# Scores and values of a unit in one place each, and k of batch 1 turned by one DMA transpose, in a fused attention and GEGLU kernel

## The chip, the cores and the metric

The kernel runs on one core of one Trainium2 chip. The metric is the device time of one execution in microseconds (us), the median of several runs. Beside it stands one profiled execution, from which all durations below come.

## The reference

Two stages follow each other. The first is attention in which each query sees its neighbours closer than 16 positions, and for each block of 32 positions one summary key (the maximum over the block) with one summary value (the mean). The second is a gated feed-forward layer over the 3072 tokens, with a gated residual.

```python
# q, k, v: 4 batches x 8 heads x 768 positions x 64
k_sum = k.reshape(B, H, nb, block, D).max(axis=3)        # block = 32, nb = 24
v_sum = v.reshape(B, H, nb, block, D).mean(axis=3)
mask_l = np.abs(pos[:, None] - pos[None, :]) < window    # window = 16
scores_s = scale * einsum(q, k_sum) + np.log(block)
a = softmax(concatenate([where(mask_l, scale * q @ k.T, -1e9), scores_s]))
x = a @ concatenate([v, v_sum])          # to 3072 tokens x 512
g, val = x @ w_gate, x @ w_val           # 512 -> 1536
ffn = (gelu(g) * val) @ w_out            # 1536 -> 512
out = x + sigmoid(x @ w_res) * ffn
```

## The kernel before

The work is cut into eight units, two per batch: a unit is half a batch's positions, thus 384 tokens (`TU`), with all 8 heads. `NP` = 4 head pairs, `HT` = 6 tiles of 64 queries (`QT`) in a unit.

**Attention.** For a tile of 64 queries the keys stand in one stationary matrix of 128 columns in `kW`: the tile's own 64 keys, 16 of the tile after, 16 of the tile before (the rims, written by `k_rims`, L245 and L246), and the 24 block maxima (`k_blocks`, L237 and L241). One matmul per tile and head gives the scores (L317). ScalarE takes their exponentials into P (L334 or L337), VectorE multiplies by a mask (L341), and a matmul with P as the stationary side gives values and the sum of weights (L355). `av_end` divides (L373, L375) into `xn`. `xt_dma` (L385) turns `xn` into `xT` by a DMA transpose; in the first two units TensorE turns it (`xt_step`).

**Feed-forward.** Twelve steps `fo_step`, one for each 128 of the 1536 columns: four matmuls g and four vv (L395), a Gelu on ScalarE (L400) and a product on VectorE (L401) into `gvT`. Then `res_step` (r, L433, with a Tanh, L436) and `ffn_step` (f, L443), and `end_step` writes the output rows from the SP queue (L456).

**Order.** The order on each engine is the order of the program text, written out by hand. While unit u ends (`mid_out`, in unit 0 `first_out`), the attention of unit n = u + 1 is interleaved with its r and f: two head pairs of scores, r, a third of f, two pairs of values, two of scores, more of f, two of values. `s_step(n, hp)` does one head pair; its scores take two PSUM banks with 384 of 512 columns used. The names `ps_mm` (4 banks), `ps_s` (2), `ps_t` and `ps_o` (1 each) are the PSUM pools; `MM2` and `TO2` name pairs of banks.

**Preparing the next batch.** Loads that change float32 to bfloat16 are issued from POOL (GpSimd), in order; a DMA waits until the one eight before it has landed. For batches 2 and 3, k is loaded with positions on the partitions (`load_k_nat`, eight DMAs, L121), turned by one DMA transpose from the SP queue (`turn_k`, L131), and POOL writes the rims of all pairs at once. For batch 1, k is loaded by one DMA (`load_k`, L89) and turned on TensorE at the first step of unit 1 (`turn_all`, 64 small transposes, L220); ScalarE places it (`k_place`, L252) and VectorE writes blocks and rims, a pair at a time at steps 0, 2, 4, 6. In unit 1, step 5, SP turns q of batch 1 (`turn_q`, L136), TensorE sums v over blocks (`vsum_grp`, L290), ScalarE copies the sums to `vpart` (L294), POOL issues four small DMAs to `vsum` (L296) and copies them into the value tiles (`vsum_bc`, L302).

Of the kernel before, what the change touches and what calls it, by code (L numbers as in the profile page):

```python
# [8 lines left out]
F32 = mybir.dt.float32  # L9
BF16 = mybir.dt.bfloat16  # L10
# [5 lines left out]
def kernel(  # L16
# [11 lines left out]
    nc = tc.nc  # L28
# [25 lines left out]
    wpool = ctx.enter_context(tc.tile_pool(name="wpool", bufs=1))  # L54
    qk = ctx.enter_context(tc.tile_pool(name="qk", bufs=1))
    work = ctx.enter_context(tc.tile_pool(name="work", bufs=3))
    ppool = ctx.enter_context(tc.tile_pool(name="ppool", bufs=4))
    upool = ctx.enter_context(tc.tile_pool(name="upool", bufs=2))
    ps_mm = ctx.enter_context(tc.tile_pool(name="ps_mm", bufs=4, space=bass.MemoryType.PSUM))
    ps_s = ctx.enter_context(tc.tile_pool(name="ps_s", bufs=1, space=bass.MemoryType.PSUM))  # L60
# [17 lines left out]
    q_nat = const.tile([128, NQ, DM], BF16, name="q_nat")  # L78
    vext = [const.tile([128, NT, H, VP], BF16, name=f"vext{i}") for i in range(2)]
    vsum = [const.tile([128, DM], BF16, name=f"vsum{i}") for i in range(2)]  # L80
    vpart = const.tile([128, DM], BF16, name="vpart")
    w_gate = wpool.tile([128, KO, DFF], BF16, name="w_gate")
    w_val = wpool.tile([128, KO, DFF], BF16, name="w_val")
# [55 lines left out]
    with tc.manual_schedule():  # L139
# [182 lines left out]
        def s_step(u, hp, st, banks=None, tiles=None):  # L322
            if tiles:
                s, banks = tiles, True
            elif banks:
                s = [p.tile([128, 512], F32, tag=tag, name="s") for p, tag in banks]
            else:
                s2 = ps_s.tile([128, 2, 512], F32, tag="s", name="s")
                s = [s2[:, hh] for hh in range(2)]
            s_mm(u, hp, [x[:, 0:TU] for x in s])  # L330
            P = ppool.tile([128, 2, HT, QT], BF16, tag="P", name="P")
            if banks:
                for hh in range(2):
                    nc.scalar.activation(P[:, hh].rearrange("p t q -> p (t q)"), s[hh][:, 0:TU], AF.Exp,  # L334
                                         scale=scale, bias=bias_t[:])
            else:
                nc.scalar.activation(P.rearrange("p a t q -> p a (t q)"), s2[:, :, 0:TU], AF.Exp,  # L337
                                     scale=scale, bias=bias_t[:])
            if u:
                Pf = P.rearrange("p a t q -> p (a t) q")  # L340
                nc.vector.tensor_mul(Pf, Pf, maskt.unsqueeze(1).to_broadcast([128, 2 * HT, QT]))  # L341
            st["P", hp] = P

        MM2 = ((ps_mm, "mm"),) * 2
        TO2 = ((ps_t, "t"), (ps_o, "ao"))
# [31 lines left out]
        def xt_step(u, ko, st, pool, tag, copy=nc.vector.tensor_copy):  # L377
            xp = pool.tile([128, TU], BF16, tag=tag, name="xp")
            for sub in range(NSUB):
                nc.tensor.transpose(xp[:, sub * 128:(sub + 1) * 128],  # L380
                                    st["xn"][:, ko, sub, :], ident[:])
            copy(st["xT"][:, ko, :], xp[:])

        def xt_dma(ko, st):
            nc.sync.dma_start_transpose(out=st["xT"][:, ko].rearrange("d (s k) -> d s k", k=128),  # L385
                                        in_=st["xn"][:, ko].rearrange("p s d -> p (s d)"))
# [6 lines left out]
        def gv_mm(ps, w, st, fo, kos):  # L393
            for ko in kos:
                nc.tensor.matmul(ps[:, 0:TU], w[:, ko, fo * 128:(fo + 1) * 128], st["xT"][:, ko, :],  # L395
                                 start=(ko == 0), stop=(ko == KO - 1), skip_group_check=True)

        def gv_end(gvT, fo, g, vv):
            ge = work.tile([128, TU], F32, tag="ge", name="ge")
            nc.scalar.activation(ge[:], g[:, 0:TU], AF.Gelu)  # L400
            nc.vector.tensor_mul(gvT[:, fo, :], ge[:], vv[:, 0:TU])  # L401

        def mm_tile(name):
            return ps_mm.tile([128, 512], F32, tag="mm", name=name)
# [13 lines left out]
            gv_end(gvT, 0, g, vv)  # L418

        def fo_last_two(st, gvT):  # L420
            g = [mm_tile("g"), mm_tile("g")]
            for i in range(2):
                gv_mm(g[i], w_gate, st, FO - 2 + i, range(KO))
            for i in range(2):
                vv = mm_tile("vv")
                gv_mm(vv, w_val, st, FO - 2 + i, range(KO))
                gv_end(gvT, FO - 2 + i, g[i], vv)

        def res_step(st, sub):
            ss = slice(sub * 128, (sub + 1) * 128)  # L430
# [117 lines left out]
        xt_step(0, 2, st, **t_turn)  # L548
        gv_part(0, 1)
        gv_mm(gv[1][0], w_gate, st, 1, (0, 1))  # L550
        xt_step(0, 3, st, **o_turn)
        gv_part(0, 2)
        gv_mm(gv[1][1], w_val, st, 1, (0, 1))
        gv_part(0, 3)
# [27 lines left out]
        def pool_after(x):  # L582
            nc.gpsimd.tensor_copy(gate2[:], x)
# [31 lines left out]

        def mid_out(u, st, gvT, nst):
            n = u + 1
            other = dict(pool=ps_t, tag="t")
            s_step(n, 0, nst)
            s_step(n, 1, nst, TO2)  # L620
            res_step(st, 0)
            res_step(st, 1)
            ffn_step(st, gvT, 0, 0, 4)
            av_step(n, 0, nst)
            xt_dma(0, nst)
            av_step(n, 1, nst, **other)
            xt_dma(1, nst)
            s_step(n, 2, nst)
            s_step(n, 3, nst, MM2)
            if n % 2 == 0:  # L630
                pool_after(nst["P", 3][0:1, 0, 0, 0:1])
                for i in range(2, 4):
                    vsum_bc(n // 2, 3 * i, 3 * i + 3, nc.gpsimd)
            ffn_step(st, gvT, 0, 4, FO)
            ffn_step(st, gvT, 1, 0, 3)
            av_step(n, 2, nst)
            xt_dma(2, nst)
            av_step(n, 3, nst, **other)
            xt_dma(3, nst)
            end_step(u, st, 0)  # L640
            ffn_step(st, gvT, 1, 3, FO)
            res_step(st, 2)
            end_step(u, st, 1)
            ffn_step(st, gvT, 2, 0, FO)
            end_step(u, st, 2)
# [9 lines left out]
        for u in range(NU):  # L655
            b, half = u // 2, u % 2
            nb = b + 1
            if half == 0 and nb == 1:
                k_sb[nb] = k_tile()
                load_k(nb, k_sb[nb], 0, 1)  # L660
                v_loads(nb)
                load_q_nat(nb)
            if u:
                gvT = upool.tile([128, FO, TU], BF16, tag="gvT", name="gvT")
            for fo in range(0 if u else 2, FO):
                if u == 0 and fo == 2:
# [24 lines left out]
                if half == 1 and nb < B:  # L691
                    if fo == 0:
                        v_rims(nb, 0, HT)
                        if nb > 1:
                            pool_after(st["xT"][0:1, KO - 1, 0:1])
                            load_q_nat(nb)
                    if fo == (5 if nb == 1 else 1):
                        turn_q(nb, 0)
                        turn_q(nb, 1)
                        vsum_grp(nb, ps_t, "t")  # L700
                        for i in range(2):
                            vsum_bc(nb, 3 * i, 3 * i + 3, nc.gpsimd)
                    if nb == 1:
                        if fo == 0:
                            tk = turn_all(k_sb[nb])
                        if fo in (0, 2, 4, 6):
                            hp = (2, 0, 1, 3)[fo // 2]
                            k_place(nb, hp, tk[hp])
                    elif 2 <= fo < 2 + NP:
                        k_blocks(nb, fo - 2)  # L710
            if u == NU - 1:
                last_out(u, st, gvT)
            else:
                nst = new_unit()
                (mid_out if u else first_out)(u, st, gvT, nst)
                st = nst

# [29 lines left out]
```

The softmax here doesn't subtract the row's maximum and nothing guards it: scores larger than these inputs give would overflow.

## Time and profile before

| what | value |
|---|---|
| median of 3 runs | 256.26 us (256.26 to 256.71) |
| the profiled execution | 256.39 us |
| its span, first to last instruction | 254.6 us |
| mean granted TensorE clock | 0.998 |
| TensorE (PE) matmul busy | 246.6 us, 97% |
| VectorE (DVE) busy | 159.4 us, 63% |
| ScalarE (ACT) busy | 129.6 us, 51% |
| GpSimd (POOL) busy | 97.3 us, 38% |
| DMA moved | 29.34 MB, mean 115 GB/s |

Times inside the span count from its first instruction. PE is the matmul row, PEld the weight loads beside it. A line such as "L443 PE MATMUL f<-w_out,gvT" means: line 443, engine, operation, what is written and from what. "Idle before" is the time in which that engine had nothing to do ahead of the instruction, and the name behind the arrow is what ended it. An engine that is not the bottleneck may be idle at no cost.

### The profile page before, as it was taken

The numbers are of one execution on the slowest core, as the hardware profiler recorded it, in microseconds if no ns is written. First come the engines' busy times: TensorE is split into PE (matmuls) and PEld (weight loads), VectorE is DVE, ScalarE is ACT, GpSimd is POOL, SyncE is SP. The second block draws the span as 40 slices with busy tenths as digits, with TensorE's granted clock in tenths as the row PEclk, the third lists the DMA queues.
The fourth block names the chain that finished last, engine by engine and source line by source line (L and its number), as shares of the span: only waits on it lengthen the run. The fifth ranks groups of instructions, "written<-read, shape, count | busy, mean of one in ns | idle before, by whom it ended". The sixth has DMA issues, their size and how long they took to land.

```text
span 254.6 us, 5847 instructions
## 1 busy us (share of the span) xinstructions
PE 246.6 (97%) x2303; PEld 139.7 (55%) x2328; DVE 159.4 (63%) x364; ACT 129.6 (51%) x216; POOL 97.3 (38%) x128
## 2 busy tenths in 40 slices
PE   6999999999999999999999999999999999999994
PEld 2676555565545665446544665446545555456544
DVE  6985796397667544858567544958567544854424
ACT  8885468366572337353572337254572337353320
POOL 8895542361506970274406970274404000000000
PEclk9999999999999999999999999999999999999999
DMA  5999999999404999399404999289604400230003
GB/s 80 177 182 197 197 205 207 175 176 222 61 19 121 159 150 150 56 161 171 103 18 120 162 155 153 49 162 170 104 18 115 98 3 0 50 139 0 3 1 124
DMA packets 98107, 29.34 MB, mean 115 GB/s; under 512 B 83224, under 2 KB 94944, under 8 KB 97984
## 3 DMA queue, kind: packets, MB, share of 16 engines
q0 software_dynamic: 68352, 14.76, 66.3%
q1 hardware_dynamic: 29728, 14.21, 25.7%
q8 instruction: 18, 0.29, 0.5%
q14 instruction: 9, 0.07, 0.1%
HBM read 29.36 MB, written 6.29 MB: 140 GB/s over the span
## 4 chain that ended last, share of the span: by engine, by line
PE 93%; DVE 5%; issue 2%; DVEq 0%
PE g L395 25%; PE vv L395 24%; PE f L443 23%; PE r L433 8%; PE s L317 3%; PE ao L355 3%; PE vs L282 1%; PE ao L367 1%; PE tp L220 1%; PE vs L290 1%; DVE ks L237 1%; PE xp L380 1%; DVE o L452 1%; DVE th L449 1%; PE gv L395 1%
## 5 line engine op out<-in xcount | busy, mean ns | idle before, releaser
L401 DVE TENSOR_TENSOR gvT<-ge,vv 128x384 bf16<-128x384 f32 x95 | 52.2, 552 | 48.1 <-PE vv L395 43.9
L400 ACT ACTIVATE ge<-g 128x384 f32<-128x384 f32 x95 | 46.7, 491 | 67.3 <-DVE gvT L401 34.8
L395 PE MATMUL g<-xT,w_gate 128*128 128x384 bf16 x380 | 78.0, 326 | 0.0
L395 PE MATMUL vv<-xT,w_val 128*128 128x384 bf16 x380 | 77.8, 326 | 0.0
L443 PE MATMUL f<-w_out,gvT 128*128 128x512 bf16 x262 | 62.7, 379 | 1.5 <-issue 1.1
L395 PEld LDWEIGHTS <-w_gate 128*128 128x128 bf16 x384 | 37.1, 98 | 26.2 <-issue 1.4
L395 PEld LDWEIGHTS <-w_val 128*128 128x128 bf16 x384 | 37.6, 98 | 24.7
L443 PEld LDWEIGHTS <-gvT 128*128 128x128 bf16 x276 | 25.7, 98 | 29.5
L107 POOL DMA_DIRECT2D vext<-in_v_dram x32 | 24.1, 777 | 15.0 <-DMA w_out<-in_moe_w_out_dram 5.6
L436 ACT ACTIVATE th<-r 128x512 f32<-128x512 f32 x24 | 13.5, 607 | 27.6 <-PE r L433 27.6
L449 DVE SCALAR_TENSOR_TENSOR th<-th,f 128x512 f32<-128x512 f32 (+2 forms) x26 | 16.6, 640 | 14.4 <-PE f L443 14.4
L341 DVE TENSOR_TENSOR P<-P,maskt 128x768 bf16<-128x768 bf16 x28 | 16.2, 580 | 11.0 <-ACT P L337 6.1
L433 PE MATMUL r<-w_res,xT 128*128 128x512 bf16 x88 | 22.7, 380 | 0.4
L302 POOL COPY vext<-vsum 32x1536 bf16<-32x1536 bf16 x12 | 17.2, 1464 | 13.0 <-DMA vsum<-vpart 12.9
L452 DVE SCALAR_TENSOR_TENSOR o<-th,xn 128x512 f32<-128x512 f32 (+2 forms) x26 | 18.2, 701 | 0.9
L375 DVE TENSOR_TENSOR xn<-ao,rz 128x384 bf16<-128x384 f32 x32 | 17.8, 557 | 1.1
L337 ACT ACTIVATE P<-s,bias_t 128x768 bf16<-128x768 f32 x17 | 15.3, 901 | 4.5 <-PE s L317 4.3
L127 POOL DMA_DIRECT2D q_nat<-in_q_dram x18 | 15.8, 899 | 0.9 <-issue 0.7
L334 ACT ACTIVATE P<-s,bias_t 128x384 bf16<-128x384 f32 x30 | 15.7, 579 | 0.0
L237 DVE TENSOR_REDUCE ks<-kW 128x24 bf16<-128x768 bf16 x16 | 15.1, 943 | 0.0
L433 PEld LDWEIGHTS <-xT 128*128 128x128 bf16 x96 | 8.8, 98 | 9.9
L373 DVE RECIPROCAL rz<-ao 128x6 f32<-128x6 f32 x32 | 6.1, 191 | 10.9 <-PE ao L355 10.0
(90 smaller groups left out, 187.1 us busy)
## 6 DMA issues: line engine op xcount, KB each, us to landing
out_dram<-o SPq DMA_DIRECT2D x23, 256.0 KB, 2.2
vext<-in_v_dram POOLq DMA_DIRECT2D x32, 96.0 KB, 6.4
q_nat<-in_q_dram POOLq DMA_DIRECT2D x18, 128.0 KB, 6.4
w_gate<-in_moe_w_gate_dram POOLq DMA_DIRECT2D x6, 256.0 KB, 8.9
w_val<-in_moe_w_val_dram POOLq DMA_DIRECT2D x6, 256.0 KB, 9.3
w_out<-in_moe_w_out_dram POOLq DMA_DIRECT2D x3, 512.0 KB, 14.4
k_nat<-in_k_dram POOLq DMA_DIRECT2D x16, 96.0 KB, 5.8
vext<-vext SPq DMA_DIRECT2D x6, 144.0 KB, 5.4
```

What stands on the lines that cost most here:

```text
L107: nc.gpsimd.dma_start(out=vext[b % 2][0:QT, :, h, 0:D], in_=v[b, h].rearrange("(t p) d -> p t d", p=QT))
L237: nc.vector.tensor_reduce(out=ks.rearrange("d (t n) -> d t n", n=2), in_=kw[:, :, 0:QT].rearrange("d t (n w) -> d t n w", w=BLK), axis=myb ...
L302: eng.tensor_copy(vext[b % 2][96:128, lo:hi, :, 0:D], src)
L341: nc.vector.tensor_mul(Pf, Pf, maskt.unsqueeze(1).to_broadcast([128, 2 * HT, QT]))
L375: nc.vector.tensor_mul(xn, ao[:, :, :, 0:D], rz.to_broadcast([128, NSUB, 2, D]))
L395: nc.tensor.matmul(ps[:, 0:TU], w[:, ko, fo * 128:(fo + 1) * 128], st["xT"][:, ko, :], start=(ko == 0), stop=(ko == KO - 1), skip_group_ch ...
L400: nc.scalar.activation(ge[:], g[:, 0:TU], AF.Gelu)
L401: nc.vector.tensor_mul(gvT[:, fo, :], ge[:], vv[:, 0:TU])
L433: nc.tensor.matmul(r[:], st["xT"][:, ko, ss], w_res[:, ko, :], start=(ko == 0), stop=(ko == KO - 1))
L443: nc.tensor.matmul(st["f", sub][:], gvT[:, fo, ss], w_out[:, fo, :], start=(fo == 0), stop=(fo == FO - 1), skip_group_check=True)
L449: nc.vector.scalar_tensor_tensor(th[:, cs], th[:, cs], 1.0, f[:, 0:n], ALU.add, ALU.mult)
L452: nc.vector.scalar_tensor_tensor(o.rearrange("p (k d) -> p k d", d=128), th[:, cs].rearrange("p (k d) -> p k d", d=128), 0.5, x, ALU.mult, ...
```

## The change

Four things are changed.

- Unit 2 and later: `mid_out` computes all scores of the next unit in one place, before r (`s_all`), and all values in one place, after the first f (`av_all`). The 24 (pair, tile) scores of a head fill banks of 512 columns: six banks in all, two each from `ps_mm`, `ps_s` and `ps_t` with `ps_o`. P becomes one tile, `p_all`, that all units share, in place of a pool of four.
- k of batch 1 is loaded as for the later batches, by eight DMAs, and turned by one DMA transpose, which SP issues at the end of unit 0's steps, ahead of `first_out`. POOL writes its rims at step 6 of unit 1, VectorE its blocks at steps 6 to 9.
- `fo_last_two` issues each Gelu behind its g in the text.
- The last `xT` copy of unit 0 goes from ScalarE to VectorE.

```diff
+    p_all = const.tile([128, 2, NP * HT, QT], BF16, name="p_all")
...
-            P = ppool.tile([128, 2, HT, QT], BF16, tag="P", name="P")
+            P = p_all[:, :, hp * HT:(hp + 1) * HT]
...
+        def s_all(u):
...
+            for i in range(3):
+                if i == 0:
+                    s = [ps_mm.tile([128, 512], F32, tag="mm", name="s") for _ in range(2)]
+                elif i == 1:
+                    s2 = ps_s.tile([128, 2, 512], F32, tag="s", name="s")
+                    s = [s2[:, hh] for hh in range(2)]
+                else:
+                    s = [p.tile([128, 512], F32, tag=tag, name="s") for p, tag in TO2]
+                for j in range(8):
+                    hp, t = divmod(8 * i + j, HT)
+                    tt = half * HT + t
+                    for hh in range(2):
+                        ps = slice(hh * 64, hh * 64 + 64)
+                        nc.tensor.matmul(s[hh][:, j * QT:(j + 1) * QT], kw[ps, tt, hp, :],
+                                         qt[ps, tt // 2, hp, (tt % 2) * QT:(tt % 2 + 1) * QT],
+                                         start=True, stop=True, skip_group_check=True)
+                js = slice(8 * i, 8 * i + 8)
+                m = maskt.unsqueeze(1).to_broadcast([128, 8, QT])
+                for hh in range(1 if i == 1 else 2):
+                    if i == 1:
+                        nc.scalar.activation(p_all[:, :, js].rearrange("p a j q -> p a (j q)"), s2[:], AF.Exp,
+                                             scale=scale, bias=bias_t[:])
+                    else:
+                        nc.scalar.activation(p_all[:, hh, js].rearrange("p j q -> p (j q)"), s[hh][:], AF.Exp,
+                                             scale=scale, bias=bias_t[:])
+                for hh in range(2):
+                    nc.vector.tensor_mul(p_all[:, hh, js], p_all[:, hh, js], m)
+
+        def av_all(u, st):
...
+            for hp in range(NP):
+                if hp < 2:
+                    pool, tag = TO2[hp]
+                    ao = pool.tile([128, NSUB, 2, D + 1], F32, tag=tag, name="ao")
+                else:
+                    if hp == 2:
+                        s2 = ps_s.tile([128, 2, 512], F32, tag="s", name="ao")
+                    ao = s2[:, hp - 2, 0:NSUB * 2 * (D + 1)].rearrange("p (s h d) -> p s h d", s=NSUB, h=2)
...
+                av_end(hp, st, ao)
+                xt_dma(hp, st)
...
         def fo_last_two(st, gvT):
-            g = [mm_tile("g"), mm_tile("g")]
+            ge = []
             for i in range(2):
-                gv_mm(g[i], w_gate, st, FO - 2 + i, range(KO))
+                g = mm_tile("g")
+                gv_mm(g, w_gate, st, FO - 2 + i, range(KO))
+                ge.append(work.tile([128, TU], F32, tag="ge", name="ge"))
+                nc.scalar.activation(ge[i][:], g[:, 0:TU], AF.Gelu)
             for i in range(2):
                 vv = mm_tile("vv")
                 gv_mm(vv, w_val, st, FO - 2 + i, range(KO))
-                gv_end(gvT, FO - 2 + i, g[i], vv)
+                nc.vector.tensor_mul(gvT[:, FO - 2 + i, :], ge[i][:], vv[:, 0:TU])
...
-        xt_step(0, 3, st, **o_turn)
+        xt_step(0, 3, st, ps_o, "ao")
...
         def mid_out(u, st, gvT, nst):
             n = u + 1
-            other = dict(pool=ps_t, tag="t")
-            s_step(n, 0, nst)
-            s_step(n, 1, nst, TO2)
+            s_all(n)
+            if n % 2 == 0:
+                pool_after(p_all[0:1, 1, 4 * HT - 1, 0:1])
+                for i in range(2, 4):
+                    vsum_bc(n // 2, 3 * i, 3 * i + 3, nc.gpsimd)
             res_step(st, 0)
             res_step(st, 1)
-            ffn_step(st, gvT, 0, 0, 4)
-            av_step(n, 0, nst)
-            xt_dma(0, nst)
-            av_step(n, 1, nst, **other)
-            xt_dma(1, nst)
-            s_step(n, 2, nst)
-            s_step(n, 3, nst, MM2)
...
-            ffn_step(st, gvT, 0, 4, FO)
-            ffn_step(st, gvT, 1, 0, 3)
-            av_step(n, 2, nst)
-            xt_dma(2, nst)
-            av_step(n, 3, nst, **other)
-            xt_dma(3, nst)
+            ffn_step(st, gvT, 0, 0, FO)
+            av_all(n, nst)
             end_step(u, st, 0)
-            ffn_step(st, gvT, 1, 3, FO)
+            ffn_step(st, gvT, 1, 0, FO)
             res_step(st, 2)
...
             if half == 0 and nb == 1:
-                k_sb[nb] = k_tile()
-                load_k(nb, k_sb[nb], 0, 1)
+                k_nat = load_k_nat(nb)
                 v_loads(nb)
                 load_q_nat(nb)
...
                         vsum_grp(nb, ps_t, "t")
                         for i in range(2):
                             vsum_bc(nb, 3 * i, 3 * i + 3, nc.gpsimd)
-                    if nb == 1:
-                        if fo == 0:
-                            tk = turn_all(k_sb[nb])
-                        if fo in (0, 2, 4, 6):
-                            hp = (2, 0, 1, 3)[fo // 2]
-                            k_place(nb, hp, tk[hp])
-                    elif 2 <= fo < 2 + NP:
-                        k_blocks(nb, fo - 2)
+                    lead = 6 if nb == 1 else 2
+                    if nb == 1 and fo == lead:
+                        k_rims(nb, slice(0, NP), nc.gpsimd)
+                    if lead <= fo < lead + NP:
+                        k_blocks(nb, fo - lead)
...
                 nst = new_unit()
+                if u == 0:
+                    turn_k(nb, k_nat)
                 (mid_out if u else first_out)(u, st, gvT, nst)
```

More of the change, by code (lines that the diff above doesn't have):

```diff
@@ L56 @@
     work = ctx.enter_context(tc.tile_pool(name="work", bufs=3))
-    ppool = ctx.enter_context(tc.tile_pool(name="ppool", bufs=4))
     upool = ctx.enter_context(tc.tile_pool(name="upool", bufs=2))
@@ L339, in s_step @@
             if u:
-                Pf = P.rearrange("p a t q -> p (a t) q")
-                nc.vector.tensor_mul(Pf, Pf, maskt.unsqueeze(1).to_broadcast([128, 2 * HT, QT]))
+                nc.vector.tensor_mul(P, P, maskt.unsqueeze(1).unsqueeze(1).to_broadcast([128, 2, HT, QT]))
             st["P", hp] = P
+        def s_all(u):
+            b, half = u // 2, u % 2
+            kw, qt = kW[b % 2], qT[b % 2]
+            s2 = None
+            for i in range(3):
[25 more added lines that the diff above has]
+                    nc.vector.tensor_mul(p_all[:, hh, js], p_all[:, hh, js], m)
@@ new lines, in av_all @@
+        def av_all(u, st):
+            b, half = u // 2, u % 2
+            for hp in range(NP):
[6 more added lines that the diff above has]
+                    ao = s2[:, hp - 2, 0:NSUB * 2 * (D + 1)].rearrange("p (s h d) -> p s h d", s=NSUB, h=2)
+                for sub in range(NSUB):
+                    for hh in range(2):
+                        for e in range(2):
+                            t = 2 * sub + e
+                            nc.tensor.matmul(ao[64 * e:64 * e + 64, sub, hh, :], p_all[:, hh, hp * HT + t, :],
+                                             vext[b % 2][:, half * HT + t, 2 * hp + hh, 0:D + 1],
+                                             start=True, stop=True, skip_group_check=True)
+                av_end(hp, st, ao)
+                xt_dma(hp, st)
@@ L617, in mid_out @@
             n = u + 1
-            other = dict(pool=ps_t, tag="t")
-            s_step(n, 0, nst)
-            s_step(n, 1, nst, TO2)
+            s_all(n)
[3 more added lines that the diff above has]
+                    vsum_bc(n // 2, 3 * i, 3 * i + 3, nc.gpsimd)
             res_step(st, 0)
             res_step(st, 1)
-            ffn_step(st, gvT, 0, 0, 4)
-            av_step(n, 0, nst)
-            xt_dma(0, nst)
-            av_step(n, 1, nst, **other)
-            xt_dma(1, nst)
-            s_step(n, 2, nst)
-            s_step(n, 3, nst, MM2)
[L630 to L633, printed above, removed]
-            ffn_step(st, gvT, 0, 4, FO)
-            ffn_step(st, gvT, 1, 0, 3)
-            av_step(n, 2, nst)
-            xt_dma(2, nst)
-            av_step(n, 3, nst, **other)
-            xt_dma(3, nst)
+            ffn_step(st, gvT, 0, 0, FO)
+            av_all(n, nst)
             end_step(u, st, 0)
-            ffn_step(st, gvT, 1, 3, FO)
+            ffn_step(st, gvT, 1, 0, FO)
             res_step(st, 2)
```

## The prediction

> **What bounds the kernel now.** I read the page first, then the chain of waits by time, then the order of work on POOL and SP, then the stretches with their DMA rate. The page says that one engine is the bound:
>
> ```profile
> PE 246.6 (97%) x2303; PEld 139.7 (55%) x2328; DVE 159.4 (63%) x364; ACT 129.6 (51%) x216; POOL 97.3 (38%) x128
> ...
> PE 93%; DVE 5%; issue 2%; DVEq 0%
> PE g L395 25%; PE vv L395 24%; PE f L443 23%; PE r L433 8%; PE s L317 3%; PE ao L355 3%; PE vs L282 1%; PE ao L367 1%; PE tp L220 1%; PE vs L290 1%; DVE ks L237 1%; PE xp L380 1%; DVE o L452 1%; DVE th L449 1%; PE gv L395 1%
> ```
>
> PE is busy 97% of the span and is 93% of the chain. Whatever DVE, ACT or POOL lose or gain costs nothing until PE waits for it. So an edit pays only by what PE executes less, and costs only by what PE waits more. The chain around the units that the change touches:
>
> ```profile
> 53.11 1.48 PE tp L220 x64
> ...
> 61.20 0.76 PE vs L290 x12
> ...
> 68.56 1.30 PE vv L395 x8
> 69.86 0.46 PE s L317 x24
> 70.32 0.32 PE r L433
> 70.64 0.05 issue
> ```
>
> Columns are start, duration, what. The 64 transposes of k (53.11) are PE work of 1.48 us, and the first weights behind them take 0.76 instead of 0.65. At 61.20 come the block sums of v for batch 1; at 69.86 the scores of unit 2, the first to read k of batch 1. And from a score step to full-width matmuls PE loses time: here r takes 0.32 and 0.05 of "issue" against 0.22 for one r, and later
>
> ```profile
> 73.51 0.46 PE s L317 x24
> 73.97 0.16 issue
> 74.13 2.32 PE f L443 x10
> ```
>
> 0.16 with no wait that the profile shows. The trace of unit 3 repeats it at 102.3.
>
> POOL in order of time (start, duration, what; in brackets the idle time before):
>
> ```profile
> 30.07 1.01 POOL L89 DMA_DIRECT2D k_sb<-in_k_dram  x1 [0.59 <-DMA w_val<-in_moe_w_val_dram]
> ...
> 62.88 2.04 POOL L296 DMA_DIRECT2D vsum<-vpart  x4 [7.67 <-ACT vpart L294]
> 67.53 2.88 POOL L302 COPY vext<-vsum 32x1536 bf16<-32x1536 bf16 x2 [2.60 <-DMA vsum<-vpart]
> ```
>
> k of batch 1 is one DMA at 30.07. After the sums, POOL issues four vsum DMAs (62.88 to 64.92), waits 2.60 us for their landing, and copies until 70.41. Later batches show what the rims of k cost on POOL:
>
> ```profile
> 103.29 0.86 POOL L245 COPY kW<-kW 128x704 bf16<-128x704 bf16 x1 [8.33 <-DMA kW<-k_nat]
> 104.10 1.09 POOL L246 COPY kW<-kW 128x704 bf16<-128x704 bf16 x1
> ```
>
> 0.86 and 1.09, thus 1.95 us. SP's transpose of k for batch 2, and the DMA stretches (the last two columns are DMA busy us and GB/s):
>
> ```profile
> 93.70 5.81 SPq L131 DMA_TRANSPOSE kW<-k_nat  x1
> ```
> ```profile
> 48.70:54.30 5.60, 5.44 (x98) 3.60 (x98) 4.00 (x8) 2.74 (x5) 5.09 (x6) 1.00 2.43 150
> 54.30:62.20 7.90, 7.90 (x68) 4.42 (x63) 7.62 (x20) 4.82 (x9) 0.91 (x2) 1.00 1.69 220
> ...
> 97.00:103.20 6.20, 5.99 (x95) 3.28 (x96) 3.79 (x9) 5.55 (x9) 0.00 (x0) 1.00 0.97 125
> ```
>
> The transpose takes 5.81 us of SP's queue and 9.5 us to landing. Loads of v and q alone move 150 GB/s (first stretch); beside the outputs of unit 0 all queues together move 220; in the tail of the k transpose, with v loads still open, 125.
>
> [...] of the two v loads issued beside the k transpose (93.47 and 94.20) the later took 8.8 us to land against 6.6 for four before it, and the packets of POOL's queue all but stop from 96.5 to 100. [...] the first warm-up matmuls take 622 ns in the median against 379 later, and after the last matmul (251.28)
>
> ```profile
> 252.00:254.60 2.60, 0.00 (x0) 0.00 (x0) 0.00 (x0) 0.00 (x0) 0.00 (x0) 0.83 0.26 81
> ```
>
> the granted clock (the column after POOL) is a mean 0.83 in 2.6 us, which is half clock for the last 0.9.
>
> **The change, part by part.**
>
> *Transposes of k gone.* PE: 1.48 + 0.11 = **-1.59 us**, on the path. Four ACT copies (0.79 each) and DVE's eight rim copies (0.2 each) go too; both engines wait for PE there, so nothing.
>
> *k of batch 1 by eight loads and a transpose.* The POOL queue is served in order: k_sb, issued at 30.07, lands at 48.7, 18.6 us later, after the last w_out (28.73 + 16.1 = 44.8). Eight loads like those of v wait in the same place, each issued when the DMA eight before has landed, the last at 45.07 as v's seventh is now. Then 0.79 MB at 150 GB/s: landed at 50.3, against 48.7. POOL's seven more issues (0.79 each) push v and q to 45.8-57 instead of 32-55; the data behind them is later still, so that is hidden, and it would cost at most 2 us if not. At 50.4 the transpose enters SP's queue *ahead* of the three outputs of unit 0 (52.69 now), the rims of v and both transposes of q: outputs move to 56.3. As in batch 2 its packets come 2.5 us later and hold the loads for some 6 us, in which they do 1 us of work: v, otherwise landed at 50.3 + 5.2 = 55.5, lands at about 60. PE wants v at 61.20 - 1.59 = 59.6: a wait of 0 to 1.
> q is 0.79 MB more, beside 0.79 MB of outputs, and the first q transpose holds its tail: the last q lands at 66.5 to 70, now 62.2. I take 68.5.
>
> *The rims of k on POOL, after the vsum copies.* This is the step that decides. POOL executes in order: sums, vsum DMAs, their landing, two copies, and only then rims for all four head pairs, which every score matmul of unit 2 reads. Floor: sums start at 59.6, vsum copies then start 6.33 later as now (67.53 - 61.20), 65.9; + 2.88 + 1.95 = **70.8**. With the vsum DMAs queued behind q (they landed 0.9 after the last q in batch 2, 122.7): 68.5 + 0.9 + 0.2 + 2.88 + 1.95 = **74.4**. PE has finished the last vv at 69.86 - 1.59 = 68.3 and stands until then, 6 us; against before, unit 2 starts 74.4 - 69.86 = **+4.5 us** (+0.9 to +6.0). The -1.59 is in this already. Everything on PE is behind it: r and f of unit 1 need no rims but come later in PE's order. SP's own branch (q transposed: 64 + 4.5 to 7.6) ends at 69 to 72 and is covered.
> Blocks of k on DVE, now from fo 6 to 9: the last is done 4 x (0.94 + 0.27) + 4 x 0.55 = 7.0 us after fo 6's last vv; PE is at the scores 5 x 1.3 = 6.5 after it. The wait hides that; without it, 0.5.
>
> *The clock.* [...] I take **+1.5**. Bounds: 0 [...] and 3.
>
> *Scores and values packed (units 2 to 7).* The same 48 + 48 matmuls. [...] 0.16 x 6 = **-1.0** (bounds: +0.6, if 48 small pairs run at the transposes' 23 ns instead of 19; -1.9, if the two value groups save one too). Exp: by 579 ns for 384 and 901 for 768 columns, 512 takes 0.69 and 1024 1.12: 3.9 us per unit for 4.1. Masks: six of about 0.45 (0.39 to 0.58) for four of 0.58. Counting from the last vv: exps from 0.54 (as now) to 4.4, masks to 4.9. PE does scores 0.92, [...] eight r 1.72, twelve f 2.58, values at 5.4: 0.5 us of cover. Then SP issues the four transposes of x 1.3 us apart from 5.4 + 1.23: the last at 10.5, landed 2.4 later, 12.9. PE asks for it at 13.4 (values 1.0, 24 f, 4 r, six first matmuls). Cover again 0.5; if it is gone, up to 0.5 in each of six units. Banks: r now takes those of vv, f those of scores; freed by 2 us, asked for at 2.8. POOL's gate copy on the last mask comes earlier, hidden.
>
> *The rest.* The copy of the last xT of unit 0 to DVE: 358 ns for 479, at most -0.1. One p_all for four P: rewritten a unit later, no wait. The order in the last two fo: the same instructions on each engine, nothing.
>
> **Sum**, against the profiled run (256.39; its span 254.6 and 1.8 around it; the median of the runs is 256.26): +4.5 + 1.5 - 1.0 = +5.0, 261.4, rounded to **261.5**.
>
> **Rivals.** *The short chain*: outputs and loads overlap well, vsum lands as now and rims are done at 70.8 to 72.2: +0.9 to +2.3, -1.0, clock 0 to 1: 256.3 to 258.7, 257.3 in the middle. For it: outputs and loads together moved 220 GB/s. Against: batch 2 shows the k transpose stopping loads. *The other side, faster*: rims done before 68.3, so that only -1.59 and -1.0 remain: 253.8. It decides at 68.3; against it, vsum's issue alone ends near 63.4 and 4.8 us of POOL follow, so the landing would have to take no time. *Packing loses its cover*: x late by 0.5 in six units on top: 264.5. *The transposes of k do not leave the path* is the same as the first case and not counted apart.
>
> **How the numbers follow.** Forecast 0.60 (own range 259 to 264), short chain 0.25, faster 0.05, lost cover 0.10. A measurement can tell about 0.2%, 0.5 us: of the short chain 0.07 lies within that. Faster 0.05, same 0.07, slower 0.88. The range from 257.0 to 264.5 leaves out the faster case, that 0.07 and the upper half of the last.
>
> **What would show it.** Right: the chain shows PE waiting for POOL's rim copy before unit 2's scores, near 74; POOL's rims right behind the vsum copies; granted clock under 1 after it; no issue gap before f in later units. Wrong: scores of unit 2 starting before 70, or a period from unit 3 on that is longer than the 28.19 of before (98.88 - 70.69).

## The result and the profile after

| | before | changed |
|---|---|---|
| median | 256.49 us (256.26 to 257.12) | 276.3 us (275.79 to 279.59) |
| ratio, 95% interval | 1 | 1.0795 [1.0708, 1.0882] |
| profiled execution, its span | 256.39, 254.6 us | 276.6, 274.5 us |
| mean granted TensorE clock | 0.998 | 0.981 |

The kernel is slower, as forecast, but by 20 us where I had 5: 276.3 lies above the range of 257.0 to 264.5. From the page of the changed kernel, here are the busy times, two rows of the span in 40 slices (TensorE and its granted clock), and the chain:

```profile
PE 251.0 (91%) x2264; PEld 140.2 (51%) x2264; DVE 157.7 (57%) x369; ACT 124.8 (45%) x205; POOL 103.5 (38%) x137
...
PE   7999999999097999799997999799988999799995
...
PEclk9999999999869999999999999999999999799999
...
PE 66%; DMA 20%; DVE 6%; POOL 5%; issue 2%; ACT 0%; POOLq 0%; DVEq 0%
PE f L497 20%; PE g L446 17%; PE vv L446 17%; PE r L487 7%; DMA w_out<-in_moe_w_out_dram 6%; DVE xn L426 4%; DMA w_val<-in_moe_w_val_dram 3%; DMA q_nat<-in_q_dram 3%; DMA vext<-in_v_dram 3%; DMA vsum<-vpart 3%; POOL vext L107 2%; DMA k_sb<-in_k_dram 2%; PE s L360 2%; PE ao L389 2%; DVE rz L424 1%
```

Read the PE row before any sum. It has one hole, a 0 in slice 11, ahead of unit 2: that one was forecast. Behind it a 7 (once 88) returns every four or five slices, and that was not. The clock row dips twice, behind the hole and once more near the end. In the chain TensorE falls from 93% to 66%, and "DVE xn L426", 4%, is new. The waits of TensorE (in all, times, longest) name both holes:

```profile
PE ao L389 <- DVE xn L426: 11.4, 6, 1.9
PE s L360 <- POOL kW L245: 5.8, 1, 5.8
```

The chain by time (start, duration, what) shows where each lies:

```profile
60.23 0.85 PE vs L290 x12
...
63.69 7.15 DMA vsum<-vpart
...
71.06 1.35 issue
72.41 1.48 POOL vext L302
73.89 0.05 issue
73.94 0.77 POOL kW L245
74.71 0.72 POOL kW L246
75.43 0.05 issue
75.47 1.41 PE s L360 x46
76.88 3.50 PE r L487 x8
80.38 2.59 PE f L497 x12
82.97 0.33 PE ao L389 x12
...
84.94 0.57 DVE xn L426
85.51 0.04 issue
85.55 0.38 PE ao L389 x12
85.93 2.69 PE f L497 x12
```

Down to 75.47 this is the forecast chain: sums of v, vsum, two copies, two rims, scores. Then the eight r take 3.50 us, at half clock. At 82.97 comes what I had missed: the values of the last pair are started only after a division on VectorE. POOL in order of time (in brackets the idle time before, and what ended it) shows why the rims come so late: they stand behind a wait of 6.82 us for vsum to land, and behind its copies.

```profile
71.00 2.87 POOL L302 COPY vext<-vsum 32x1536 bf16<-32x1536 bf16 x2 [6.82 <-DMA vsum<-vpart]
73.94 0.77 POOL L245 COPY kW<-kW 128x704 bf16<-128x704 bf16 x1
74.65 0.77 POOL L246 COPY kW<-kW 128x704 bf16<-128x704 bf16 x1
```

And SP's queue, where the transpose of k (L131) stands ahead of the three outputs of unit 0 and the rims of v:

```profile
50.42 5.96 SPq L131 DMA_TRANSPOSE kW<-k_nat  x1
56.45 1.51 SPq L510 DMA_DIRECT2D out_dram<-o  x3
60.04 0.62 SPq L113 DMA_DIRECT2D vext<-vext  x1
...
62.23 7.57 SPq L136 DMA_TRANSPOSE qT<-q_nat  x2
```

Last, the stretches (from and to, length, then busy time of each engine, granted clock, DMA busy and GB/s):

```profile
50.40:54.30 3.90, 3.70 (x26) 2.15 (x25) 3.33 (x7) 2.45 (x4) 3.90 (x6) 1.00 2.02 140
54.30:62.20 7.90, 7.61 (x55) 4.18 (x54) 4.04 (x8) 3.19 (x7) 3.16 (x5) 1.00 2.19 184
62.20:70.80 8.60, 6.76 (x42) 3.85 (x40) 7.26 (x14) 3.88 (x7) 1.82 (x4) 1.00 1.74 212
```

From 54.30 to 62.20 all queues move 184 GB/s where before moved 220, with the transpose of k in flight until 61.76.

**Where the 19.9 us of span are.** Unit 2's scores run from 75.47 instead of 69.86: 5.6. The clock is 0.5 from 73.39 to 80.22, and r and scores take 3.50 and 1.41 where they take 1.83 and 0.81 at full clock: 2.3. Six units have the gap of 1.89 (it ends at 85.55, 115.50, 146.30, 176.24, 207.05 and 236.99). From a unit's first value matmul to the f behind them pass 2.96 (82.97 to 85.93), where the same 48 take 0.88 without the gap (e4_packed_pairs, below): each costs 2.08. The packing saves 0.33 a unit (e4 again). Six times the difference: 10.5. A second half-clock window from 237.24 makes twelve f take 4.33 instead of 2.69: 1.6. Together 20.0.

### The profile page after: what moved, and what is told of

Same layout as the page of the kernel before. It is cut to its first block, busy times and chain, and to the rows that moved or that the text cites. A ratio compares the mean times of both kernels' runs of the same rounds, so it can differ in the third digit from the quotient of the medians.

```text
span 274.5 us, 5757 instructions
## 1 busy us (share of the span) xinstructions
PE 251.0 (91%) x2264; PEld 140.2 (51%) x2264; DVE 157.7 (57%) x369; ACT 124.8 (45%) x205; POOL 103.5 (38%) x137
## 4 chain that ended last, share of the span: by engine, by line
PE 66%; DMA 20%; DVE 6%; POOL 5%; issue 2%; ACT 0%; POOLq 0%; DVEq 0%
PE f L497 20%; PE g L446 17%; PE vv L446 17%; PE r L487 7%; DMA w_out<-in_moe_w_out_dram 6%; DVE xn L426 4%; DMA w_val<-in_moe_w_val_dram 3%; DMA q_nat<-in_q_dram 3%; DMA vext<-in_v_dram 3%; DMA vsum<-vpart 3%; POOL vext L107 2%; DMA k_sb<-in_k_dram 2%; PE s L360 2%; PE ao L389 2%; DVE rz L424 1%
## 5 line engine op out<-in xcount | busy, mean ns | idle before, releaser
L446 PE MATMUL g<-xT,w_gate 128*128 128x384 bf16 x380 | 78.0, 326 | 0.2 <-DVE th L503 0.2
L446 PE MATMUL vv<-xT,w_val 128*128 128x384 bf16 x380 | 77.8, 326 | 0.0
L451 ACT ACTIVATE ge<-g 128x384 f32<-128x384 f32 x81 | 39.8, 491 | 64.1 <-DVE gvT L452 32.4
L452 DVE TENSOR_TENSOR gvT<-ge,vv 128x384 bf16<-128x384 f32 x81 | 44.4, 552 | 39.6 <-PE vv L446 37.3
L497 PE MATMUL f<-w_out,gvT 128*128 128x512 bf16 x276 | 65.2, 386 | 0.0
L446 PEld LDWEIGHTS <-w_gate 128*128 128x128 bf16 x384 | 37.2, 98 | 26.7 <-issue 1.9
L446 PEld LDWEIGHTS <-w_val 128*128 128x128 bf16 x384 | 37.6, 98 | 24.6
L497 PEld LDWEIGHTS <-gvT 128*128 128x128 bf16 x276 | 26.7, 100 | 32.1 <-issue 2.7
L503 DVE SCALAR_TENSOR_TENSOR th<-th,f 128x512 f32<-128x512 f32 (+2 forms) x26 | 16.7, 642 | 23.6 <-PE f L497 23.6
L487 PE MATMUL r<-w_res,xT 128*128 128x512 bf16 x96 | 24.7, 400 | 0.0
L373 DVE TENSOR_TENSOR p_all<-p_all,maskt 128x512 bf16<-128x512 bf16 x36 | 14.2, 423 | 14.6 <-ACT p_all L370 10.7
L121 POOL DMA_DIRECT2D k_nat<-in_k_dram x24 | 18.6, 806 | 10.5 <-DMA w_out<-in_moe_w_out_dram 5.4
L426 DVE TENSOR_TENSOR xn<-ao,rz 128x384 bf16<-128x384 f32 x32 | 17.8, 557 | 1.1
L370 ACT ACTIVATE p_all<-s,bias_t 128x512 bf16<-128x512 f32 x24 | 15.3, 693 | 6.6 <-PE s L360 6.6
L506 DVE SCALAR_TENSOR_TENSOR o<-th,xn 128x512 f32<-128x512 f32 (+2 forms) x26 | 16.9, 651 | 0.9
L389 PE MATMUL ao<-vext,p_all 128*64 128x65 bf16 x288 | 6.8, 196 | 11.4 <-DVE xn L426 11.4
```

What stands on the lines that cost most here:

```text
L121: nc.gpsimd.dma_start(out=k_nat[:, :, h * D:(h + 1) * D], in_=k[b, h].rearrange("(t p) d -> p t d", p=QT))
L426: nc.vector.tensor_mul(xn, ao[:, :, :, 0:D], rz.to_broadcast([128, NSUB, 2, D]))
L487: nc.tensor.matmul(r[:], st["xT"][:, ko, ss], w_res[:, ko, :], start=(ko == 0), stop=(ko == KO - 1))
L497: nc.tensor.matmul(st["f", sub][:], gvT[:, fo, ss], w_out[:, fo, :], start=(fo == 0), stop=(fo == FO - 1), skip_group_check=True)
L503: nc.vector.scalar_tensor_tensor(th[:, cs], th[:, cs], 1.0, f[:, 0:n], ALU.add, ALU.mult)
L506: nc.vector.scalar_tensor_tensor(o.rearrange("p (k d) -> p k d", d=128), th[:, cs].rearrange("p (k d) -> p k d", d=128), 0.5, x, ALU.mult, ...
```

## Experiments

Ratios are to the kernel before, timed on the same chip. My theory after the result: pairs 2 and 3 of the values lie in one PSUM tile of two banks (`s2` in `av_all`), and the wait on it is kept for the whole tile. So pair 3's matmuls wait for the division that reads pair 2, and VectorE comes to that only after the divisions of pairs 0 and 1. The rival: VectorE, with masks before the divisions, is behind in any case. For k: the POOL order and v's delay as forecast, against the packed scores as the cause.

**e1_pairs.** In `av_all`, all 48 matmuls ahead of the divisions of pairs 2 and 3:

```diff
-                av_end(hp, st, ao)
-                xt_dma(hp, st)
+                if hp < 2:
+                    av_end(hp, st, ao)
+                    xt_dma(hp, st)
+                else:
+                    late.append((hp, ao))
+            for hp, ao in late:
+                av_end(hp, st, ao)
+                xt_dma(hp, st)
```

> The changed kernel, with one order altered in the packed values: the matmuls of pairs 2 and 3 come first, and the divisions of both behind them. Shared tile (my theory now): pairs 2 and 3 write two halves of one tile, and the wait is kept for the whole tile, so that pair 3's first matmul waits until VectorE has divided pair 2, which stands behind pairs 0 and 1; the gap of 1.89 us in six units goes (11.3 us), and the second cold stretch near 237 us (1.6) with it: 276.3 - 12.9 = 263.4. Rival, VectorE is too slow for four pairs in a row in any case and PE will wait later, for x or for a bank: the gap moves into the next first step g and the time stays above 270.

262.89 us, 1.0238 [1.0224, 1.0252]. The six gaps are gone, and so is the second half-clock window; 13.4 of the 20 us are back. The stop before unit 2 stays (scores at 74.11 and 74.83), with a half clock from 72.73 to 79.56.

**e9_own_bank** puts the rival to the test without a change of order: matmuls and divisions as in the changed kernel, only pair 3 lies in a tile of its own.

```diff
+                elif hp == 2:
+                    s2 = ps_s.tile([128, 2, 512], F32, tag="s", name="ao")
+                    ao = s2[:, 0, 0:NSUB * 2 * (D + 1)].rearrange("p (s h d) -> p s h d", s=NSUB, h=2)
                 else:
-                    if hp == 2:
-                        s2 = ps_s.tile([128, 2, 512], F32, tag="s", name="ao")
-                    ao = s2[:, hp - 2, 0:NSUB * 2 * (D + 1)].rearrange("p (s h d) -> p s h d", s=NSUB, h=2)
+                    ao = ps_mm.tile([128, NSUB, 2, D + 1], F32, tag="mm", name="ao")
```

> The changed kernel, with one edit: the sums of value pair 3 go to a bank of ps_mm instead of the second half of the two-bank tile that holds pair 2. Order of matmuls and divisions as in the changed kernel. Theory (pair 3's matmuls wait for pair 2's division because both lie in one tile, for which the wait is kept as a whole): the six gaps of 1.89 us ahead of pair 3 go, and the time is that of the altered value order, 262.9 (262.3 to 263.6). Rival (VectorE is simply behind with the masks and divisions and TensorE would wait for it in any bank): the gaps stay or move to the first f, which then waits for a bank: 270 to 276.

263.76 us, 1.0285 [1.0257, 1.0314]: 0.2 above what I had expected at most, and far from the rival. TensorE, in order of time, in this kernel:

```profile
82.18 0.95 PE L390 MATMUL ao<-vext,p_all 128*64 128x65 bf16 x48
83.06 2.76 PE L498 MATMUL f<-w_out,gvT 128*128 128x512 bf16 x11
```

and TensorE and VectorE in the changed kernel (in brackets the idle time before, and what ended it):

```profile
82.90 0.76 PE L389 MATMUL ao<-vext,p_all 128*64 128x65 bf16 x36
...
84.94 0.56 DVE L426 TENSOR_TENSOR xn<-ao,rz 128x384 bf16<-128x384 f32 x1
85.55 0.38 PE L389 MATMUL ao<-vext,p_all 128*64 128x65 bf16 x12 [1.89 <-DVE xn L426]
```

36 matmuls, a wait for pair 2's division, 12 more; with its own tile all 48 in one go. VectorE does the same divisions in the same order, so it is the tile and not VectorE's load. The two pairs lie in different banks of the shared tile, and pair 3 waited 1.89 all the same; in e9 the 48 are done at 83.13, ahead of pair 2's division at 84.22.

**e2_packed and e3_k** split the change: e2 keeps the packed part and takes k of batch 1 as before; e3 is the kernel before with the k part alone. The edit of e2, which e3 makes the other way round on the kernel before:

```diff
-                k_nat = load_k_nat(nb)
+                k_sb[nb] = k_tile()
+                load_k(nb, k_sb[nb], 0, 1)
...
-                    lead = 6 if nb == 1 else 2
-                    if nb == 1 and fo == lead:
-                        k_rims(nb, slice(0, NP), nc.gpsimd)
-                    if lead <= fo < lead + NP:
-                        k_blocks(nb, fo - lead)
+                    if nb == 1:
+                        if fo == 0:
+                            tk = turn_all(k_sb[nb])
+                        if fo in (0, 2, 4, 6):
+                            hp = (2, 0, 1, 3)[fo // 2]
+                            k_place(nb, hp, tk[hp])
+                    elif 2 <= fo < 2 + NP:
+                        k_blocks(nb, fo - 2)
...
-                if u == 0:
-                    turn_k(nb, k_nat)
```

> The changed kernel with k of batch 1 loaded by one DMA and turned by TensorE as in the kernel before; scores and values stay packed as in the change. Theory: the late start of unit 2 (5.6 us) and the cold clock behind it (2.3) go, the six gaps of 1.89 stay: 276.3 - 7.9 = 268.4[...]. Rival, the packing itself delays unit 2: over 272.

> The kernel before with the k of batch 1 alone changed: eight loads, one DMA transpose, rims on GpSimd at step 6. Theory: unit 2 starts 5 to 6 us late, near 75, and the clock halves for 2 to 7 us of it, with 2.3 us lost: 256.5 + 5.6 + 2.3 = 264.4. Rival, the late start comes from the packing, which needs all four pairs' k at once where the kernel before needs two: with two pairs first the same rims are needed (one copy writes all pairs), so I expect no relief; if the rival holds, under 260.

e2: 270.25 us, 1.0507 [1.0479, 1.0536], 1.9 above expectation. All six gaps are there; the rest are two half-clock windows, from 78.35 and from 170.51, where my 268.4 had one. The number of such windows changes from run to run: the fastest of e2's four took 268.36 us at a mean clock of 0.994, the others at least 270.21 at 0.987 (half of 3.41 us is 0.006 of the span). e3: 263.4 us, 1.0247 [1.023, 1.0264], 1.0 under expectation. Unit 2's scores start at 69.78 in e2 and, with none of them packed, not before 74.0 in e3: the late start is the k part's. So both parts cost, and they nearly add: against the kernel before as timed with them (256.69), 13.6 and 6.7 make 20.3, where the whole change cost 19.8.

**e4_packed_pairs**: packed scores and the altered value order, thus the two diffs of e1 and e2 together.

> The kernel before with scores and values packed, the values in the altered order (matmuls of pairs 2 and 3 ahead of both divisions), k of batch 1 as before. Theory: 48 scores in one place take 0.81 and the r behind them 0.11 more than its eight matmuls, against 0.46 + 0.15 + 0.46 + 0.16 in two places: 0.31 less in each of six units, thus 256.5 - 1.9 = 254.6. Rival, the last transposed x (landed about 12.9 us after the last vv, asked for at 13.4) is late and takes it back: 256.5 or more, with a wait ahead of the last g of the first step.

254.6 us, 0.9927 [0.9907, 0.9948]: **faster than both kernels**, by 0.7% of the kernel before. Its chain, around the values of unit 2:

```profile
69.86 0.81 PE s L360 x48
70.67 0.32 PE r L494
70.99 0.05 issue
71.04 1.46 PE r L494 x6
72.50 2.59 PE f L504 x12
75.09 0.88 PE ao L390 x48
75.97 0.16 issue
76.13 2.54 PE f L504 x11
```

One score group takes 0.81 for two of 0.46, and one set of values 0.88 for two of 0.50. The period from unit 2 to unit 3 is 97.72 - 69.86 = 27.86 against 28.19. (The 0.16 called issue is a matmul that the trace lacks: behind it stand 11 f of 12. More of this below.)

**e8_small**: e4 with the Gelu order of `fo_last_two` and the last `xT` copy as before.

```diff
-            ge = []
+            g = [mm_tile("g"), mm_tile("g")]
...
-        xt_step(0, 3, st, ps_o, "ao")
+        xt_step(0, 3, st, **o_turn)
```

> As e4_packed_pairs, with the last two steps of the gate and the last xT copy of unit 0 as in the kernel before. Both theories: no difference beyond 0.1 us from e4_packed_pairs (254.6); the copy on VectorE could be worth at most 0.1.

254.58 us, 0.993 [0.9917, 0.9944]: these two edits are worth nothing.

**e5_rims**: e1 with the rims of k on POOL ahead of the vsum copies.

```diff
                         vsum_grp(nb, ps_t, "t")
+                        if nb == 1:
+                            k_rims(nb, slice(0, NP), nc.gpsimd)
...
-                    if nb == 1 and fo == lead:
-                        k_rims(nb, slice(0, NP), nc.gpsimd)
```

> The changed kernel with the altered order of the values (as in e1_pairs), and the rims of k of batch 1 on GpSimd ahead of the two vsum copies instead of behind them. Theory: the rims wait for the k transpose alone (landed at 61.3 in e1_pairs) and for GpSimd's four DMA issues, so they are done near 66; PE then waits for the transpose of q, landed at 70.6 in e1_pairs: unit 2 starts near 70.8 instead of 74.8 (-4.0), [...] (-2.3), thus 262.9 - 6.3 = 256.6. Rival, the late q and k together set the start whatever GpSimd's order: 262.

257.61 us, 1.0059 [1.003, 1.0089]: 5.3 us below e1, so POOL's order was most of the late start; with it went the half clock, as I had estimated (1.000 throughout), worth 2.3 of the 5.3 (e6, below). It stays 1.0 above expectation. VectorE, POOL and TensorE of this kernel:

```profile
63.74 1.75 DVE L241 COPY kW<-ks 128x288 bf16<-128x288 bf16 x1
63.90 0.78 POOL L245 COPY kW<-kW 128x704 bf16<-128x704 bf16 x1
...
66.00 0.81 PE L453 MATMUL vv<-xT,w_val 128*128 128x384 bf16 x4 [0.57 <-DVE gvT L459]
...
66.85 0.23 DVE L241 COPY kW<-ks 128x288 bf16<-128x288 bf16 x1
...
70.34 0.70 PE L360 MATMUL s<-qT,kW 64*128 64x64 bf16 x36 [0.64 <-DMA qT<-q_nat]
...
71.59 0.35 PE L360 MATMUL s<-qT,kW 64*128 64x64 bf16 x12 [0.55 <-DVE kW L241]
```

VectorE's block copy takes 0.23 us alone and 1.75 beside POOL's two rim copies: it ends at 65.49, POOL at 65.39. TensorE waits 0.57 for the product behind it, and 0.55 for another such copy, of 1.50 us beside a vsum copy of POOL. Why VectorE's copies take longer there, no run shows. The scores then wait for q (0.64), no longer for POOL.

**e6_warm and e10_shift** ask what the clock is worth. e6 is e1 with 24 matmuls of 512 columns on a constant tile ahead of unit 2's scores; e10 has 48 of 256 columns, the same time in more instructions.

```diff
+            if n == 2:
+                keep_warm(24)
             s_all(n)
```

> The changed kernel with the altered order of the values, and 24 warm-up matmuls of 216 ns (results unused) ahead of the scores of unit 2: 5.2 us of work in the 5.5 us in which PE waits. Theory: the start of unit 2 stays near 74.8, the clock stays full, and the 2.3 us lost between 74.8 and 79.6 come back: 262.9 - 2.3 = 260.6. Rival, the half clock costs little there because ScalarE and VectorE set the pace behind the scores: 262.5 to 263.

> The altered value order with 48 warm-up matmuls of 256 columns ahead of the scores of unit 2, in place of 24 of 512: the same TensorE work in twice as many instructions, so every later instruction of TensorE stands 24 places further on in its stream. Both theories: full clock, scores of unit 3 near 102.6. Theory (the waits for x before g, 2.2 us in all with 24 warm-ups, come from x transposes that meet a fetch of instructions, whose phase moves with the stream): the waits change place and size by over half, and the time lies between 260.4 and 262.0. Rival (the waits belong to the earlier restart of TensorE, which leaves x too little time): the same waits within 0.3 us, 262.6.

Both run at clock 1.000, with unit 3's scores at 102.64 and 102.92 instead of 104.94. In e10 unit 2 also starts 0.26 later; from the second start of unit 2's scores (74.83 in e1) to unit 3's pass 27.89 in both, and 30.17 in e1. So the half clock had cost 2.3. But e6 took 262.56 us, 1.0221 [1.0202, 1.0241], 2.0 above expectation, and e10 259.94, 1.0126 [1.0098, 1.0155]. In e6 TensorE waits for x five times, where in e1 it did twice for 0.5 in all (in all, times, longest):

```profile
PE g L453 <- DMA xT<-xn: 2.2, 5, 0.9
```

In e10 that wait is gone, and the time is below even what I had expected there. So it doesn't belong to the earlier restart. The trace has a DMA queue for instructions, which moves blocks of 16 KB (in e10 18 of them, 0.29 MB). In e6 five of these fetches start at 109.3, 138.5, 168.9, 196.7 and 229.0, each while a transpose of x is under way, and seven transposes that they met take 3.0 to 4.3 us to landing instead of 2.3. In e10 the corresponding five start at 109.3, 137.8, 166.1, 194.9 and 222.8, within 0.4 us of the first transpose of a unit, and none takes over 2.9. In all twelve traces together, 70 transposes of x had a fetch in flight and took 2.3 to 4.3 us, 52 of them over 2.5; of the 218 others all but one took at most 2.4. That the fetch causes the delay fits all this; but no run moves a fetch and nothing else, so it is not shown.

**e7_knat** asks what delays v and q: k of batch 1 by the eight loads of the change, but turned on TensorE, 48 transposes of 64 columns, in the faster e4; VectorE writes blocks and rims pair by pair, as in the kernel before.

```diff
+            for hp in range(NP):
+                for t in range(NT):
+                    nc.tensor.transpose(tps[hp][:, t, :], k_nat[:, t, hp * 128:(hp + 1) * 128], ident[0:QT, 0:QT])
...
+                        if fo == 0:
+                            tk = turn_nat(k_nat)
```

> Scores and values packed in the altered order (as in e4_packed_pairs), with k of batch 1 loaded by the eight DMAs of the change but turned by TensorE, 48 transposes of 64 x 128 in place of 64 of 96 x 64; no DMA transpose of k. What it tells apart: were it the loads in small rows that made v and q late, v would land at 59.5 and q at 69 as in e1_pairs; if it is the DMA transpose, v lands near 55.4, q near 63. Time by the second: [...]254.6 - 0.5 = 254.1; by the first, PE waits for v and q at unit 2 and it is 256 or more.

255.22 us, 0.9944 [0.9931, 0.9956]. With the same loads the last v lands at 55.29 and the last q at 64.86; with the DMA transpose (e1) at 59.87 and 69.27. It is the transpose that holds the loads. My expected gain of 0.5 us over e4 was wrong: 48 transposes take 1.50 us in the chain (31 ns each), as long as the 64 of before (1.48, 23 ns each).

## Why the prediction was wrong

The account in runs, between neighbours that differ in one thing: packing with the altered order 254.6 - 256.5 = -1.9; late k, at the full clock that e10's warm-up keeps, 259.94 - 254.6 = +5.3; half clock, with 0.5 of waits for x, 262.89 - 259.94 = +2.95; pairs 2 and 3 in one tile, 276.3 - 262.89 = +13.4. Sum +19.8. (The runs come from four occasions, on which the kernel before had medians of 256.35 to 256.69; so each term is sure to some 0.3.)

**The step that failed** is the packing's count "values 1.0, 24 f, 4 r": I took the 48 value matmuls as one run without a wait. They take 0.76, wait 1.89, then 0.38, in all 2.96 up to the next f where I had 1.0. The prediction priced banks that r and f take over from vv and scores, but not the one inside `av_all`, where pair 3 takes the second half of a tile while VectorE still reads the first. It was in the diff: one `tile` call for two pairs, and `av_end` between their matmuls. Rows of before, of TensorE's chain and of VectorE, would have priced it:

```profile
73.01 0.50 PE ao L355 x24
```
```profile
73.37 0.20 DVE L373 RECIPROCAL rz<-ao 128x6 f32<-128x6 f32 x1 [0.53 <-PE ao L355]
...
74.07 0.18 DVE L373 RECIPROCAL rz<-ao 128x6 f32<-128x6 f32 x1
```

A division starts 0.36 after its pair's first value matmul and takes 0.70 with its reciprocal, so the third is done 0.36 + 2.1 = 2.46 after the first matmul; 36 matmuls take 1.5 x 0.50 = 0.75. That leaves a wait of 1.7 in six units, 10 us. Of the rivals, the one that came nearest in place was the packing that loses its cover, but through x and at 0.5; there was no wait for x in the changed kernel. My sign of error, "a period from unit 3 on that is longer than the 28.19", is what came, though the periods must be compared like with like, as every second one holds the sums of v: from unit 4 to unit 5 the scores are 168.36 - 138.43 = 29.93 apart, in the kernel before 155.23 - 127.04 = 28.19. That the kernel is slower was foreseen for the late k alone: by itself (e3) it cost 6.7, against 4.5 + 1.5 in the prediction. Two thirds of the loss came from the other part, which I had as a gain.

**The clock**, +1.5 with 0 to 3, was my estimate; what the profile of before shows is a half clock from 253.70 on, 2.4 us after the last matmul (251.28). Measured in the changed kernel: TensorE stood for 5.80 us, from 68.96 to 74.76, and the clock was 0.5 from 73.39 to 80.22. That cost 2.3, the upper half, and a second window cost 1.6 that the prediction could not have, since it had no stop there.

**The late start of unit 2**, +4.5: right in mechanism and nearly in size. k landed at 50.15 (50.3), the last v at 59.77 (about 60), the last q at 68.31 (68.5), TensorE's wait at the sums was 0.29 (0 to 1). Only the last of vsum was 2.5 after q, not 0.9, and so the rims ended at 75.4, not 74.4. In e1 the 0.9 held (69.27, 70.19), and scores came at 74.11 and 74.83.

**The transposes of k gone**, -1.59: TensorE ended the last vv at 68.96, 0.9 earlier than before; 0.29 of the rest went to the wait at the sums, and 0.37 at 53.26, where the second g of unit 1, which had stood behind the transposes, now waits for VectorE ("PE g L446 <- DVE th L503") and starts 1.02 after the vv before it instead of 0.65. As the prediction has it, it then stood still, so nothing of this was gained.

**The packing without its fault**, -1.0 in all (0.16 a unit): measured -0.33 a unit, -1.9 in all, at the end of its bounds. The 0.16 was misread as the price of the step from scores to f. In the kernel before, f has 276 weight loads and 262 matmuls on record: in the pause a matmul is missing. From 73.97 to 76.45 the program has 11 f; at 0.216 each (twelve in 2.59) they take 2.37 of the 2.48, so the step from small to full-width matmuls costs 0.11. The same 0.11 shows where all are on record. Four r elsewhere take 0.86, thus eight 1.72; behind the scores of unit 7 of the changed kernel they take 1.83:

```profile
229.98 1.83 PE r L487 x8
```

A unit has three such steps before and two in e4: 0.11. 48 scores in one go take 0.11 less than two groups of 24, and 48 values 0.12 less. Together that is the 0.33, of which the prediction had only the step.

**The small parts**, at most 0.1: 0.02 in e8, not to be told from nothing. **Faster**, with 5%: right to be small for this kernel; e4 shows that the faster result needed k of batch 1 left alone and the values in another order.

## What to carry to other kernels

For each tile that holds two results, ask when the second is written and when the first is read: here the wait was kept for the whole tile of two banks and cost 1.89 us in each of six units, so issue all writes before the first read, or give each its own tile. An instruction that many later steps need should not stand in an engine's program behind a wait for a DMA's landing, 6.82 us of it on POOL in the changed kernel; moving the rims ahead of it gave 5.3 us from e1 to e5, the half clock that it spared included. And a change in two parts is first run in its two parts: the packed scores and values gain 0.7% once the k part is out and the values are in an order that doesn't wait.

## What the runs showed of the hardware

**One stop of 1.89 us in six was followed by half clock.** In these traces the clock changes of a run lie on a grid of 3.413 us (in the changed kernel 80.22 to 237.24 is 46 of them). The window ahead of the fall at 73.39 (69.97 to 73.39) holds no work of TensorE; the one ahead of the fall at 237.24 holds 1.52 us of it. Here are two windows of the changed kernel that each hold a gap of 1.89 us (columns as in the stretches above, TensorE's busy time behind the length):

```profile
83.63:87.05 3.42, 1.53 (x20) 0.87 (x18) 2.85 (x8) 0.00 (x0) 0.00 (x0) 1.00 0.24 50
233.83:237.24 3.41, 1.52 (x51) 1.01 (x49) 2.07 (x6) 0.29 (x1) 0.00 (x0) 1.00 0.10 19
```

After the second the clock fell to 0.5, after the first not, at the same busy time. Of f alone the first holds 1.19 us and the second 0.58; the rest are the small value matmuls. In e2 the two windows before its half clock hold 1.36 us of TensorE, 0.29 of it f. That the small matmuls count for less than full-width ones of the same busy time is my estimate from these figures, and not shown. Not every window of mostly small ones is followed by half clock: one of e2 from 105.66 to 109.07, with 0.97 of f and 0.69 of values, is followed by full clock, and so is one of the kernel before from 14.77 to 18.18, with 3.03 us of almost only small matmuls. In the kernel before, the window from 250.29 to 253.70 holds only 0.99 us of short f and is followed by half clock. These few windows are a pattern, not a proof, and give no threshold.

**Equal work of TensorE, different times.** The same TensorE time in 24 or 48 instructions gave 262.56 and 259.94 us in kernels that are otherwise the same. Differences of 1% between kernels with as little cover for x as here need a second look at which transposes were slow.
